# Regrouping the attention bursts between the units of a feed-forward pass: eight bursts instead of ten, value products behind score bursts, paired transposes in batch 1

## The chip, the cores and the metric

The kernel runs on one core of a Trainium2 chip. The metric is the device time of one execution in microseconds (us); lower is better.

## The reference

Two layers follow each other. The first is attention over 8 batches of 8 heads, 576 tokens and 64 values a head, with a mask: a token sees the tokens within 32 positions of it, eight global tokens are seen by all, and the global tokens see all. The second is a gated feed-forward layer on the 4608 tokens with 512 columns and 1536 hidden columns.

```python
def _attn_ref(q, k, v, global_idx):
    scores = scale * np.matmul(q, k.transpose(0, 1, 3, 2))
    mask = np.abs(pos[:, None] - pos[None, :]) <= window      # window = 32
    mask = mask | is_global[:, None] | is_global[None, :]
    scores = np.where(mask, scores, -1000000000.0)
    ...
    return np.matmul(attn, v)

def _moe_ref(x, w_gate, w_val, w_out):
    g = x @ w_gate
    silu = g * (1.0 / (1.0 + np.exp(-g)))
    return silu * (x @ w_val) @ w_out
```

## The kernel before

**The feed-forward part sets the pace.** It works on nine chunks of 512 tokens. A chunk is 16 units, written out by `ffn`: twelve gate units (four matmuls with `wg_sb`, four with `wv_sb`, each 128x512; then ScalarE's tanh and two VectorE products that make `h`), and four output units (twelve matmuls into `po`, a copy to `osb` by ScalarE, and a store). The loop at the end of the kernel runs through all units and counts them with `n`. Behind unit `n` it emits whatever stands in `gaps[n]`. In this text such a place is a **slot**, and what is emitted there on TensorE is a **burst**. The schedule is manual: every engine executes in the order in which the program emits.

**The attention of batch b is a list of steps** in `attention(b)`, dealt out to slots.

- `step_T` transposes k and q of two heads on TensorE (batches 1 and 2; from batch 3 on `transpose_qk` does it with DMA transposes on SP's queue).
- `step_GT`, `step_S2`, `step_SG`, `step_P2T` and `step_AV2` are the parts for the global tokens. `step_P2T` transposes on TensorE, and for batches 4 to 7 (`b >= XP`) with a DMA on SP's queue.
- `step_S(u)`, "score u", u = 0 to 4: sixteen small matmuls into `ps_s` (eight for u = 4), the exponential `pe` on ScalarE, and the mask product `pt` on VectorE.
- `step_AV(tp)`, "value tp", tp = 0 to 3: two matmuls with `gvt` and sixteen with `va` and its copy `vb`, shifted by 64 rows, into `ps_av`. Then VectorE normalises (`den`, its reciprocal, and the product `xa`). Values 0 and 1 use the masks of scores 0 and 1, values 2 and 3 those of scores 2 and 3. `step_AV8`, the tail product, does the last 64 tokens with score 4.
- `step_X(tp)` brings `xa` into `xT`, the input of the feed-forward part: four TensorE transposes and a ScalarE copy for batches 0 and 1, a DMA transpose on SP's queue from batch 2 (`b >= XB`). `step_X8` does so for the tail.

`vb()` copies `va` into `vb` with two DMAs on SP's queue, at the fourth place of batch 1's list, which is slot 5. They wait for the loads of v, which GpSimd issues in the order of the program.

**PSUM.** The pools `psc` (tag "sc") and `pm` (tag "m") hold one tile each, of 4 KB a partition[...]. Whoever takes the tile next waits until its last reader is done. [...] In `step_S` score 4 of batch 2 takes `pm`, the other scores after batch 0 take `psc`. `step_AV` places the values:

```python
            elif b < XQ:
                pool, tag = (psc, "sc") if tp and (b < XB or tp % 2) else (pm, "m")
            else:
                pool, tag = pm, "m"
```

**Where the steps land.** Batch 1 starts its list at slot 2, batch 2 at slot 15, one group a slot. Score 2 is then at slot 9 in batch 1 and at slot 22 in batch 2. Batches 3 to 7 deal their ten groups (one of them empty) over a whole chunk, group i in slot `o + 1 + (16 * i) // 10`, with `o = 16 * (b - 1)`: counted from `o`, score 2 is at 9, score 3 with value 0 at 10, value 1 at 12, score 4 with value 2 at 13, value 3 with the tail at 15. Slots 0 to 11 follow gates, slots 12 to 15 follow outputs.

Of the kernel before, what the change touches and what calls it, by code (L numbers as in the profile page):

```python
# [10 lines left out]
BF16 = mybir.dt.bfloat16  # L11
# [6 lines left out]
P = 128  # L18


def bc(ap, dims):

    return bass.AP(tensor=ap.tensor, offset=ap.offset, ap=[ap.ap[0]] + dims)
# [3 lines left out]
def kernel(  # L27
# [11 lines left out]
    nc = tc.nc  # L39

    B, H, S, D = q.shape
# [8 lines left out]
    HP = H // 2  # L50
# [4 lines left out]
    XB = 2  # L55
    XP = 4
# [11 lines left out]
    work = ctx.enter_context(tc.tile_pool(name="work", bufs=2))  # L68
# [3 lines left out]
    psc = ctx.enter_context(tc.tile_pool(name="psc", bufs=1, space=bass.MemoryType.PSUM))  # L72
    pm = ctx.enter_context(tc.tile_pool(name="pm", bufs=1, space=bass.MemoryType.PSUM))
# [73 lines left out]
    ident = const.tile([P, P], BF16)  # L147
# [23 lines left out]
    def clear(i):  # L171
# [10 lines left out]
        out=oh16.rearrange("p h a r -> p (h a r)"),  # L182
        in_=ident.rearrange("p (a g) -> p a g", g=NG), axis=AX.X, op=ALU.add,
# [3 lines left out]
        out=p8, in_=ident.rearrange("p (a g) -> p g a", g=NG), axis=AX.X, op=ALU.add  # L187
# [11 lines left out]
        out=tmp8h, in0=dmask.rearrange("p h r -> p (h r)"), in1=i8_f, op=ALU.mult  # L199
# [4 lines left out]
        out=gidx_f, in_=gidx_i64.bitcast(I32).rearrange("p (a b) -> p a b", b=2)[:, :, 0]  # L204
# [8 lines left out]
        out=hrow, in0=hrow, scalar1=float(S), scalar2=gcol, op0=ALU.mult, op1=ALU.add  # L213
# [4 lines left out]
        out=mka, in_=oh16.rearrange("p h a r -> p a r h"), axis=AX.X, op=ALU.add  # L218
# [6 lines left out]
        out=thr, in0=asel, scalar1=R2 + 0.25, scalar2=-0.25, op0=ALU.mult, op1=ALU.add  # L225
# [3 lines left out]
        out=sgn, in0=asel, scalar1=2.0, scalar2=-1.0, op0=ALU.mult, op1=ALU.add  # L229
# [3 lines left out]
        out=thi, in0=asel[:, 0:1], scalar1=1e6, scalar2=0.5, op0=ALU.mult, op1=ALU.add  # L233
# [25 lines left out]
    xT = wpool.tile([P, NCC, NT], BF16)  # L259

    def load_wgv(i):
# [13 lines left out]
        out=band, in_=band, compare_op=ALU.is_ge, fill=0.0,  # L275
# [3 lines left out]
        out=band, in_=band, compare_op=ALU.is_ge, fill=0.0,  # L279
# [60 lines left out]
    def attention(b):  # L340
        kT = kT_bufs[b % 2]
        va = va_bufs[b % 2]
        st = {}
# [139 lines left out]

        def step_S(u):
            hg, t0 = ((0, 0), (1, 0), (0, 4), (1, 4), (None, 8))[u]
            pool, tag = (pm, "m") if b == 0 and u in (2, 3) or b == 2 and u == 4 else (psc, "sc")
            ps = pool.tile([P, 2, 512], FP32, tag=tag, name="ps_s")
            if hg is None:
                slots = [(hp, hp, 8) for hp in range(HP)]
            else:  # L490
                slots = [(4 * i + tl, 2 * hg + i, t0 + tl) for i in range(2) for tl in range(4)]
            for slot, hp, t in slots:
                for par in range(2):
                    r = 64 * par
                    nc.tensor.matmul(  # L495
                        out=ps[:, par, 64 * slot : 64 * slot + 64],
                        lhsT=kT[r : r + 64, hp, 64 * t : 64 * t + P],
                        rhs=qTs[b][r : r + 64, hp, 64 * t : 64 * t + 64],
                        start=True, stop=True,
                    )  # L500
            ns = len(slots)
            pe = ppool.tile([P, 2, ns, 64], BF16, tag="pe", name="pe", bufs=3)
            nc.scalar.activation(  # L503
                out=pe, in_=ps[:, :, 0 : 64 * ns].rearrange("p r (s c) -> p r s c", c=64),
                func=AF.Exp, scale=SCALE,
            )
            pt = ppool.tile([P, 2, ns, 64], BF16, tag="p", name="pt")
            st["p", u] = pt
            mult = lambda: nc.vector.tensor_tensor(  # L509
                out=pt.rearrange("p r s c -> p (r s) c"),  # L510
                in0=pe.rearrange("p r s c -> p (r s) c"),
                in1=bc(band, [[0, 2 * ns], [1, 64]]), op=ALU.mult,
            )
            if b == 0:
                st["p*", u] = mult
            else:
                mult()
# [16 lines left out]
            )  # L534

        def step_AV(tp):
            st["xa", tp] = work.tile([P, H, D], BF16, tag="xa", name="xa", bufs=3)
            if b == 0:
                pool, tag = (pm, "m") if tp % 2 else (psc, "sc")
            elif b < XQ:  # L540
                pool, tag = (psc, "sc") if tp and (b < XB or tp % 2) else (pm, "m")
            else:
                pool, tag = pm, "m"
            full = pool.tile([P, 2, 512], FP32, tag=tag, name="ps_av")
            ps = full[:, :, 0 : 4 * W].rearrange("p g (h c) -> p g h c", c=W)
            for hg in range(2):
                r = slice(64 * hg, 64 * hg + 64)
                nc.tensor.matmul(  # L548
                    out=ps[:, hg], lhsT=st["pg"][r, P * tp : P * tp + P],
                    rhs=st["gv"][r].rearrange("p h r c -> p (h r) c"),  # L550
                    start=True, stop=False, skip_group_check=True,
                )
            for hg in range(2):
                pt = st["p", 2 * (tp // 2) + hg]
                for hl in range(4):
                    for e in range(2):
                        nc.tensor.matmul(  # L557
                            out=ps[64 * e : 64 * e + 64, hg, hl, :],
                            lhsT=pt[:, hl % 2, 4 * (hl // 2) + 2 * (tp % 2) + e, :],
                            rhs=(va if e == 0 else st["vb"])[:, tp, 4 * hg + hl, :],  # L560
                            start=False, stop=(hl == 3), skip_group_check=True,
                        )
            if b == 0:
                st["xa*", tp] = lambda: normalise(ps, st["xa", tp], 8)
            else:
                normalise(ps, st["xa", tp], 8)
# [25 lines left out]
        def step_X(tp):  # L592
# [18 lines left out]
            c0 = S * b + P * tp  # L611
            nc.scalar.copy(out=xT[:, :, c0 : c0 + P], in_=ps)

        def step_X8():
            if b >= XB:
                c0 = S * b + 512
                for g in range(2):
                    nc.sync.dma_start_transpose(
                        out=xT[:, 2 * g : 2 * g + 2, c0 : c0 + 64],
                        in_=st["xa8"][64 * g : 64 * g + 64].rearrange("p h d -> p (h d)"),  # L620
                    )
                return
            ps = mtile([P, 2, P], BF16, "ps_x8")
            for i in range(2):
                nc.tensor.transpose(
                    out=ps[:, i, :],
                    in_=st["xa8"][:, 2 * i : 2 * i + 2, :].rearrange("p h d -> p (h d)"),
                    identity=ident,
                )
            c0 = S * b + 512  # L630
            nc.scalar.copy(
                out=xT[:, :, c0 : c0 + 64].rearrange("p (g i) c -> p i g c", g=2),
                in_=ps.rearrange("p i (g c) -> p i g c", g=2),
            )
# [11 lines left out]
        L = lambda f, *a: (lambda: f(*a))  # L646
        if b == 0:
# [19 lines left out]
            [L(step_S2), L(step_SG)],  # L667
            [L(step_P2T), L(step_S, 0)],
            [L(step_S, 1), L(step_AV2)],
            [L(step_S, 2)],  # L670
            [L(step_S, 3), L(step_AV, 0)],
            [L(step_AV, 1), L(step_X, 0)],
            [L(step_AV, 2), L(step_X, 1)],
            [L(step_AV, 3), L(step_X, 2)],
            [L(step_X, 3), L(step_S, 4)],
        ]
        end = [[L(step_AV8)], [L(step_X8)]]
        if b < XQ:
            return [
# [1 line left out]
                *([[L(step_T, 2)], [L(step_GT), L(step_T, 3), vb]] if b == 1 else  # L681
                  [[L(step_GT), L(step_T, 2)], [L(step_T, 3), vb]]),
            ] + mid + end
        return [
            [L(step_GT), vb],
            [L(step_S2), L(step_SG)],
            [L(step_S, 0), L(step_P2T)],
            [],
            [L(step_S, 1), L(step_AV2)],
            [L(step_S, 2)],  # L690
            [L(step_S, 3), L(step_AV, 0), L(step_X, 0)],
            [L(step_AV, 1), L(step_X, 1)],
            [L(step_S, 4), L(step_AV, 2), L(step_X, 2)],
            [L(step_AV, 3), L(step_AV8), L(step_X, 3), L(step_X8)],
        ]


    def ffn(t0, n):
# [102 lines left out]
    gaps = {i: [] for i in range(9)}  # L801
# [23 lines left out]
    for b in range(XQ, B):  # L825
        steps = attention(b)
        o = 16 * (b - 1)
        for i, g in enumerate(steps):
            slot = o + 1 + (16 * i) // len(steps)
            gaps[slot] = gaps.get(slot, []) + g  # L830
        if b > XQ:
            tr_at[b] = o - 16 + 5
        if b > 4:
            cast_at[b] = o - 32 + 8
        v_at[b] = o - 16 + 2
        g_at[b] = o - 16 + 6
        m_at[b] = o - 16 + 13
# [4 lines left out]
    n = 0  # L842
# [38 lines left out]
```

## Time and profile before

| | |
|---|---|
| median of 11 runs | 369.67 us (367.06 to 370.54) |
| the profiled execution: its time | 365.74 us |
| the profiled execution: span of its instructions | 364.0 us |
| TensorE matmul busy | 346.1 us, 95% |
| VectorE busy | 233.8 us, 64% |
| ScalarE busy | 153.1 us, 42% |
| GpSimd busy | 97.4 us, 27% |

The profile is one execution. Busy times are unions of an engine's instructions, and matmuls overlap in their pipeline, so the cost of a group of matmuls is read from the end of the group before to its own end. A wait is an idle stretch of an engine with the instruction that ended it. In the timeline rows the columns are start, duration, engine, line, operation, what it writes and reads, and how many were merged into the row.

### The profile page before, as it was taken

The page shows a single profiled execution, that of the slowest core. Times are in us where ns is not written, and L with a number is a line of the kernel's source. Part 1 is how long each engine was busy: PE and PEld are TensorE (multiplying, and loading weights), DVE is VectorE, ACT ScalarE, POOL GpSimd, SP SyncE. Part 2 cuts the span into 40 slices and gives each one's busy share as a digit, 9 for nine tenths or more (in the row PEclk, how much of TensorE's full clock was granted, in tenths as well). Part 3 has the DMA queues.
Part 4 walks back from the last instruction along what each step waited for, and adds up shares of the span by engine and source line. Part 5 has one row for each costly group of instructions (what it writes and reads, how often), then busy time and mean ns, then how long its engine had stood idle before and what let it go on. Part 6 is the DMA issues. An engine that isn't in the chain of part 4 may idle for free.

```text
span 364.0 us, 7818 instructions
## 1 busy us (share of the span) xinstructions
PE 346.1 (95%) x3177; PEld 170.9 (47%) x3226; DVE 233.8 (64%) x469; ACT 153.1 (42%) x238; POOL 97.4 (27%) x114
## 2 busy tenths in 40 slices
PE   3769999999999999999999999999999999999996
PEld 2546544554444444444444444444444444444444
DVE  6665786368934884588548854885488638724850
ACT  5635673467324551355225532552254333323322
POOL 7925545934544001540245024100000000000000
PEclk9989999999999999999999999999999999999999
DMA  7999999999999927999899998932350131011002
GB/s 105 137 207 204 134 191 200 178 202 134 155 167 201 176 52 116 138 153 162 140 135 139 141 150 145 167 68 60 115 87 0 45 117 23 0 59 59 0 14 104
DMA packets 141636, 43.51 MB, mean 120 GB/s; under 512 B 126368, under 2 KB 135840, under 8 KB 141600
## 3 DMA queue, kind: packets, MB, share of 16 engines
q0 software_dynamic: 93824, 19.40, 62.7%
q1 hardware_dynamic: 47776, 23.60, 31.3%
q8 instruction: 25, 0.41, 0.5%
q14 instruction: 11, 0.09, 0.1%
HBM read 38.28 MB, written 15.34 MB: 147 GB/s over the span
## 4 chain that ended last, share of the span: by engine, by line
PE 92%; DMA 3%; DVE 2%; issue 1%; ACT 1%; POOL 0%; POOLq 0%; SPq 0%
PE pg L713 26%; PE po L774 25%; PE pv L713 25%; PE ps_s L495 3%; PE ps_av L557 3%; DMA vb<-va 2%; PE ps_av L548 1%; PE ps_t L377 1%; DMA k_bf<-in_k_dram 1%; PE ps_av L464 1%; PE ps_s L429 1%; PE po L761 1%; PE pg L731 1%; PE ps_x L606 1%; PE pv L731 1%
## 5 line engine op out<-in xcount | busy, mean ns | idle before, releaser
L713 PE MATMUL pg<-xT,wg_sb 128*128 128x512 bf16 x389 | 106.0, 380 | 2.0 <-issue 0.3
L713 PE MATMUL pv<-xT,wv_sb 128*128 128x512 bf16 x415 | 107.2, 379 | 0.3
L746 DVE SCALAR_TENSOR_TENSOR gv<-th,pg 128x512 bf16<-128x512 bf16 x107 | 73.3, 685 | 40.1 <-ACT th L744 39.5
L744 ACT ACTIVATE th<-pg 128x512 bf16<-128x512 f32 x107 | 63.9, 598 | 79.0 <-PE pg L713 70.2
L774 PE MATMUL po<-wo_sb,h 128*128 128x512 bf16 x410 | 92.8, 379 | 1.2 <-issue 1.0
L750 DVE TENSOR_TENSOR h<-gv,pv 128x512 bf16<-128x512 bf16 x107 | 73.6, 688 | 11.5 <-PE pg L713 0.5
L713 PEld LDWEIGHTS <-wv_sb 128*128 128x128 bf16 x424 | 41.5, 98 | 50.0
L774 PEld LDWEIGHTS <-h 128*128 128x128 bf16 x420 | 39.9, 98 | 46.4
L102 POOL DMA_DIRECT2D va<-in_v_dram x40 | 35.2, 988 | 95.6 <-PE ps_av L557 87.1
L713 PEld LDWEIGHTS <-wg_sb 128*128 128x128 bf16 x424 | 37.0, 98 | 40.9 <-issue 1.7
L779 ACT ACTIVATE osb<-po 128x512 f32<-128x512 f32 x35 | 20.9, 597 | 81.3 <-PE po L774 76.4
L503 ACT ACTIVATE pe<-ps_s 128x1024 bf16<-128x1024 f32 (+1 forms) x40 | 37.5, 938 | 18.6 <-PE ps_s L495 18.6
L509 DVE TENSOR_TENSOR pt<-pe,band 128x1024 bf16<-128x1024 bf16 (+1 forms) x40 | 25.5, 638 | 20.8 <-ACT pe L503 20.3
L524 DVE TENSOR_REDUCE den<-ps_av 128x8 f32<-128x16 f32 (+1 forms) x40 | 6.7, 169 | 35.7 <-PE ps_av L557 33.2
L530 DVE TENSOR_TENSOR xa<-ps_av,den 128x512 bf16<-128x512 f32 (+1 forms) x40 | 25.5, 638 | 1.6 <-DMA xT<-xa 0.3
L495 PEld LDWEIGHTS <-kT 64*128 64x128 bf16 x576 | 11.2, 97 | 15.9 <-issue 14.8
L495 PE MATMUL ps_s<-qT,kT 64*128 64x64 bf16 x576 | 16.0, 195 | 1.1 <-ACT pe L503 1.1
L557 PE MATMUL ps_av<-vb,pt 128*64 128x66 bf16 x256 | 14.4, 199 | 1.5 <-DMA vb<-va 1.5
L557 PE MATMUL ps_av<-va,pt 128*64 128x66 bf16 x256 | 14.7, 199 | 0.0
L109 POOL DMA_DIRECT2D qf<-in_q_dram x5 | 14.0, 2801 | 0.0
L557 PEld LDWEIGHTS <-pt 128*64 128x64 bf16 x512 | 11.1, 111 | 5.8 <-DMA vb<-va 1.6
L109 POOL DMA_DIRECT2D kf<-in_k_dram x5 | 11.4, 2285 | 7.4 <-DMA qf<-in_q_dram 7.1
(123 smaller groups left out, 213.7 us busy)
## 6 DMA issues: line engine op xcount, KB each, us to landing
out_dram<-osb SPq DMA_DIRECT2D x35, 256.0 KB, 2.2
vb<-va SPq DMA_DIRECT2D x14, 264.0 KB, 4.6
va<-in_v_dram POOLq DMA_DIRECT2D x24, 128.0 KB, 18.2
kf<-in_k_dram POOLq DMA_DIRECT2D x5, 576.0 KB, 10.4
qf<-in_q_dram POOLq DMA_DIRECT2D x5, 576.0 KB, 18.3
k_bf<-in_k_dram POOLq DMA_DIRECT2D x6, 288.0 KB
q_bf<-in_q_dram POOLq DMA_DIRECT2D x6, 288.0 KB, 4.3
va<-in_v_dram POOLq DMA_DIRECT2D x16, 96.0 KB, 7.8
```

Of the source, the lines that this page charges most:

```text
L102: nc.gpsimd.dma_start(out=va[lo:hi, u, :, 0:D], in_=vs[t0 + lo : t0 + hi])
L109: nc.gpsimd.dma_start(out=t, in_=src[b].rearrange("h s d -> s h d"))
L495: nc.tensor.matmul(out=ps[:, par, 64 * slot : 64 * slot + 64], lhsT=kT[r : r + 64, hp, 64 * t : 64 * t + P], rhs=qTs[b][r : r + 64, hp, 64 ...
L503: nc.scalar.activation(out=pe, in_=ps[:, :, 0 : 64 * ns].rearrange("p r (s c) -> p r s c", c=64), func=AF.Exp, scale=SCALE,)
L509: mult = lambda: nc.vector.tensor_tensor(out=pt.rearrange("p r s c -> p (r s) c"), in0=pe.rearrange("p r s c -> p (r s) c"), in1=bc(band, ...
L530: nc.vector.tensor_tensor(out=xa.rearrange("p (g h) d -> p g h d", g=g), in0=bc(ps, pst + [[1, D]]), in1=bc(den, [[4, g], [1, 4], [0, D]]) ...
L557: nc.tensor.matmul(out=ps[64 * e : 64 * e + 64, hg, hl, :], lhsT=pt[:, hl % 2, 4 * (hl // 2) + 2 * (tp % 2) + e, :], rhs=(va if e == 0 els ...
L713: nc.tensor.matmul(out=ps[:, 0:n], lhsT=w[:, cc, P * fc : P * (fc + 1)], rhs=xT[:, cc, t0 : t0 + n], start=(cc == 0), stop=(cc == NCC - 1),)
L744: nc.scalar.activation(out=th[:, 0:n], in_=pg[:, 0:n], func=AF.Tanh, scale=0.5)
L746: nc.vector.scalar_tensor_tensor(out=gv[:, 0:n], in0=th[:, 0:n], scalar=1.0, in1=pg[:, 0:n], op0=ALU.add, op1=ALU.mult,)
L750: nc.vector.tensor_tensor(out=st["h"][:, fc, 0:n], in0=gv[:, 0:n], in1=pv[:, 0:n], op=ALU.mult)
L774: nc.tensor.matmul(out=po, lhsT=st["h"][:, fc, P * ts : P * (ts + 1)], rhs=wo_sb[:, fc, :], start=(fc == 0), stop=(fc == NFC - 1),)
```

## The change

In **batches 3 to 7** the list becomes a table of slots: eight bursts instead of nine that are not empty. Value 0 joins score 2 (slot 9), value 1 joins score 3 (slot 11), value 2 stays with score 4 (now slot 12), value 3 stays with the tail (now slot 14). The DMA transpose of `step_P2T` is emitted at slot 2 for batches 4 to 7.

In **batch 1** value 0 joins score 2 and value 1 joins score 3. A new step `step_X01(n)` transposes two `xa` tiles into one `psc` tile, and one ScalarE copy brings both to `xT`. The second such pair stands in one group with score 4. The list is one group shorter.

In **batch 2** the same merges are made, value 3 joins score 4, and the list is two groups shorter. Score 4 of batch 2 moves to `psc`. For batches 1 and 2 only value 2 takes `psc`; the other values take `pm`. The pool of `xa` has four buffers instead of three.

```diff
-            pool, tag = (pm, "m") if b == 0 and u in (2, 3) or b == 2 and u == 4 else (psc, "sc")
+            pool, tag = (pm, "m") if b == 0 and u in (2, 3) else (psc, "sc")
...
-            st["xa", tp] = work.tile([P, H, D], BF16, tag="xa", name="xa", bufs=3)
+            st["xa", tp] = work.tile([P, H, D], BF16, tag="xa", name="xa", bufs=4)
...
-                pool, tag = (psc, "sc") if tp and (b < XB or tp % 2) else (pm, "m")
+                pool, tag = (psc, "sc") if tp == 2 else (pm, "m")
...
+        def step_X01(n):
+
+            ps = psc.tile([P, 2, 2, HP, P], BF16, tag="sc", name="ps_x")
+            for i in range(2):
+                for hp in range(HP):
+                    nc.tensor.transpose(
+                        out=ps[:, i, 0, hp, :],
+                        in_=st["xa", 2 * n + i][:, 2 * hp : 2 * hp + 2, :].rearrange(
+                            "p h d -> p (h d)"
+                        ),
+                        identity=ident,
+                    )
+            c0 = S * b + 2 * P * n
+            nc.scalar.copy(
+                out=xT[:, :, c0 : c0 + 2 * P].rearrange("p h (i c) -> p i h c", i=2),
+                in_=ps[:, :, 0],
+            )
...
             [L(step_S2), L(step_SG)],
             [L(step_P2T), L(step_S, 0)],
             [L(step_S, 1), L(step_AV2)],
-            [L(step_S, 2)],
-            [L(step_S, 3), L(step_AV, 0)],
-            [L(step_AV, 1), L(step_X, 0)],
-            [L(step_AV, 2), L(step_X, 1)],
-            [L(step_AV, 3), L(step_X, 2)],
-            [L(step_X, 3), L(step_S, 4)],
+            [L(step_S, 2), L(step_AV, 0)],
+            [L(step_S, 3), L(step_AV, 1)],
+            [L(step_AV, 2)],
+            [L(step_AV, 3), L(step_X01, 0)],
+            [L(step_X01, 1), L(step_S, 4)],
+        ] if b < XB else [
+            [L(step_S2), L(step_SG)],
+            [L(step_P2T), L(step_S, 0)],
+            [L(step_S, 1), L(step_AV2)],
+            [L(step_S, 2), L(step_AV, 0), L(step_X, 0)],
+            [L(step_S, 3), L(step_AV, 1), L(step_X, 1)],
+            [L(step_AV, 2), L(step_X, 2)],
+            [L(step_S, 4), L(step_AV, 3), L(step_X, 3)],
         ]
...
-        return [
-            [L(step_GT), vb],
-            [L(step_S2), L(step_SG)],
-            [L(step_S, 0), L(step_P2T)],
-            [],
-            [L(step_S, 1), L(step_AV2)],
-            [L(step_S, 2)],
-            [L(step_S, 3), L(step_AV, 0), L(step_X, 0)],
-            [L(step_AV, 1), L(step_X, 1)],
-            [L(step_S, 4), L(step_AV, 2), L(step_X, 2)],
-            [L(step_AV, 3), L(step_AV8), L(step_X, 3), L(step_X8)],
-        ]
+        return {
+            1: [L(step_GT), vb],
+            2: [L(step_S2), L(step_SG)] + ([L(step_P2T)] if b >= XP else []),
+            4: [L(step_S, 0)] + ([] if b >= XP else [L(step_P2T)]),
+            7: [L(step_S, 1), L(step_AV2)],
+            9: [L(step_S, 2), L(step_AV, 0), L(step_X, 0)],
+            11: [L(step_S, 3), L(step_AV, 1), L(step_X, 1)],
+            12: [L(step_S, 4), L(step_AV, 2), L(step_X, 2)],
+            14: [L(step_AV, 3), L(step_AV8), L(step_X, 3), L(step_X8)],
+        }
...
-        for i, g in enumerate(steps):
-            slot = o + 1 + (16 * i) // len(steps)
-            gaps[slot] = gaps.get(slot, []) + g
+        for i, g in steps.items():
+            gaps[o + i] = gaps.get(o + i, []) + g
```

## The prediction

> **What bounds the kernel now.** I read the page first: busy time by engine, then the granted clock and the list of TensorE's waits.
>
> ```profile
> PE 346.1 (95%) x3177; PEld 170.9 (47%) x3226; DVE 233.8 (64%) x469; ACT 153.1 (42%) x238; POOL 97.4 (27%) x114
> ```
> ```profile
> PE ps_t L357 <- DMA k_bf<-in_k_dram: 6.3, 2, 6.0
> PE ps_av L557 <- DMA vb<-va: 1.5, 1, 1.5
> PE ps_g L395 <- DVE kqm L249: 1.2, 1, 1.2
> PE ps_s L495 <- ACT pe L503: 1.1, 1, 1.1
> ```
>
> TensorE is the bound: every long wait lies in the first 25 us, in batch 0. After it TensorE runs without a hole, so only two things can change the time: what a burst costs TensorE itself, and new waits. The timeline of TensorE in a later batch (start, duration) prices the bursts:
>
> ```profile
> 242.54 1.03 PE L713 MATMUL pv<-xT,wv_sb 128*128 128x512 bf16 x4
> 243.50 0.41 PE L495 MATMUL ps_s<-qT,kT 64*128 64x64 bf16 x16
> 243.84 1.04 PE L713 MATMUL pg<-xT,wg_sb 128*128 128x512 bf16 x4
> 244.72 1.03 PE L713 MATMUL pv<-xT,wv_sb 128*128 128x512 bf16 x4
> 245.68 0.41 PE L495 MATMUL ps_s<-qT,kT 64*128 64x64 bf16 x16
> ...
> 246.38 0.20 PE L557 MATMUL ps_av<-vb,pt 128*64 128x66 bf16 x1
> ...
> 248.24 2.75 PE L774 MATMUL po<-wo_sb,h 128*128 128x512 bf16 x12
> ```
>
> From end to end: a score burst alone takes 243.57 to 243.91, 0.34 us. Scores with a value product take 245.75 to 246.58, 0.83. A value product alone, after the output product ending 250.99, took to 251.59: 0.59. The gate unit behind a burst takes 1.83 (243.91 to 245.75); in a row of gates each takes 1.73. So a merge saves 0.34 + 0.59 - 0.83 = 0.10 in the burst and 0.10 in the unit behind it: **0.20 us for each burst that joins another**.
>
> [...] the 0.10 appears where 128*128 tiles give way to 64*128 or 128*64 and back. [...] the vb copies of batch 1 took 8 us beside weight loads, 4.7 in the median. [...] (busy us in the first number after the stretch, clock behind the engines):
>
> ```profile
> 21.70:25.11 3.41, 1.50 (x25) 0.95 (x26) 2.14 (x6) 0.58 (x1) 0.88 (x2) 1.00 1.22 236
> 25.11:28.52 3.41, 3.41 (x34) 2.42 (x34) 1.96 (x5) 0.58 (x1) 1.35 (x2) 0.50 1.25 204
> 18.28:21.70 3.42, 2.16 (x54) 1.45 (x54) 2.34 (x8) 2.05 (x2) 1.34 (x3) 1.00 1.16 180
> ```
>
> A window with 1.50 us busy was followed by half clock for 3.41 us; one with 2.16 was not.
>
> **The gain.** Batches 3 to 7: score 2, scores 3 with value 0 and value 1 (0.34 + 0.83 + 0.59, with 0.10 behind each) become two merged bursts: 0.20 each, 5 x 0.20 = 1.0 us. Batches 1 and 2, each burst with its 0.10 behind, in the same costs (four transposes behind a value product add 0.34 and leave no 0.10 behind them, four more 0.22; 24 transposes of q and k take 0.63, the tail product 0.48). Batch 1, score 2 to score 4: before 0.44 + 1.05 + 0.93 + 0.93 + 0.93 + 0.55 = 4.83, with a wait of 0.12 in it; after 0.93 + 0.93 + 0.69 + 1.15 + 0.76 = 4.46. Its tail steps meet batch 2's transposes elsewhere: before 1.09 + 0.84, after 0.58 + 0.84 + 0.73, so 0.22 more. Batch 2, score 2 to the tail: before 0.44 + 0.93 + 3 x 0.69 + 0.32 + 0.58 = 4.34, after 0.93 + 0.93 + 0.69 + 0.81 + 0.58 = 3.94. Net 0.37 - 0.22 + 0.40 = 0.55. Gain in all: **1.55 us**. Nothing is removed from TensorE; ACT has two copies of some 1.01 us for batch 1 (estimate: 372 ns at 256 columns and 585 at 512 give 0.83 ns a column) for four of 585. ACT is 42% busy and its copies end nothing, so 0.
>
> **New wait 1: vb of batch 1.** Its copies stay at slot 5, but value 0 moves from slot 10 to slot 9. The timeline at slot 10 and the issue on SP:
>
> ```profile
> 46.54 0.46 SPq L130 DMA_DIRECT2D vb<-va  x1
> ```
> ```profile
> DMA to landing us min/median/max: 7.9/8.0/8.0
> ```
> ```profile
> 54.51 0.22 PE L557 MATMUL ps_av<-va,pt 128*64 128x66 bf16 x1
> 54.63 0.22 PE L557 MATMUL ps_av<-vb,pt 128*64 128x66 bf16 x1
> ```
>
> The second copy lands at 46.54 + 8.0 = 54.54, and already holds the first product with vb by 0.12 us (54.51 to 54.63). The copies wait on POOL's v loads, which wait on transfers, not on TensorE, so they land no earlier. At slot 9 the burst would end at 51.95 + 0.83 = 52.78; held until 54.63 it ends at 55.07, as it does now at slot 10. **Cost 2.29 us.** Everything on TensorE queues behind it. Bounds: 0 if the copy lands by 52.5, 3 if it is 0.7 late.
>
> **New wait 2: one buffer for the transposes and score 4 of batch 1.** Before, transpose 3 is in pool pm and score 4 in psc. After, the pair X01(1) and score 4 stand in one burst and both take the single psc tile. Score 4 waits for ACT's copy, and all of TensorE for score 4. Before, at this place:
>
> ```profile
> 67.29 0.39 PE L606 MATMUL ps_x<-ident,xa 128*128 128x128 bf16 x4
> 67.49 0.60 ACT L779 ACTIVATE osb<-po 128x512 f32<-128x512 f32 x1 [2.00 <-PE po L774]
> 67.61 0.29 PE L495 MATMUL ps_s<-qT,kT 64*128 64x64 bf16 x8
> 67.98 0.58 ACT L612 COPY xT<-ps_x 128x512 bf16<-128x512 bf16 x1
> ```
>
> The copy starts 0.53 after the output product's end at 67.45 (behind osb), takes 1.01, release about 0.05: score 4 begins at +1.6 where its transposes end at +0.44. **Cost 1.15 us.** Bounds 0.9 to 1.3.
>
> **New wait 3: batch 2 with one gate between bursts.** Value 0, 1 and 3 take pm, value 2 takes psc: each waits for VectorE's normalisation of the one before. VectorE per slot: two products of a gate 1.51, mask 0.69, normalisation 1.1 = 3.3 us, against TensorE's 0.83 + 1.83 = 2.66. It falls behind. Rows of VectorE:
>
> ```profile
> 88.59 0.18 DVE L479 TENSOR_TENSOR gvt<-lo,gvt 128x4 bf16<-128x4 f32 x1
> ...
> 92.13 0.69 DVE L509 TENSOR_TENSOR pt<-pe,band 128x1024 bf16<-128x1024 bf16 x1
> ...
> 93.18 0.69 DVE L530 TENSOR_TENSOR xa<-ps_av,den 128x512 bf16<-128x512 f32 x1
> ```
>
> From mask start to xa end is 1.74 us. I carry the after order forward from slot 22 (gate end 88.53). gvt ends 88.77, value 0 wanted at 88.71: with about 0.05 us for the release, 0.1. Mask 2 from 90.07, so xa 0 ends 91.81; value 1 wanted at 91.50: 0.37. Then gate and mask again: xa 1 at 94.85, gate 24's products to 96.24, xa 2 at 97.22; score 4, in psc, wanted at 96.7: 0.5. xa 3 at 100.0; the tail product in pm wanted at 99.83: 0.2. **Cost 1.2 us**, bounds 0.6 and 1.8. Batch 1's same chain is covered by wait 1, in which VectorE catches up.
>
> **Later batches: nothing.** Two gates lie between slots 9 and 11. By the same working xa 1 ends at 251.17 and value 2, behind output product 0, is wanted at 251.55: cover 0.35 us; if gone, up to 0.3 x 5. SP's order stays vb, p2t, kT, qT, so the p2t transposes (slot 4 to 2) issue as now; the last transposes pass one store in later batches and two in batch 2, six osb buffers hide it. POOL's order is unchanged. The fourth xa buffer takes a wait off VectorE (0.3 us, off the path). An empty list entry costs 0.
>
> **Sum:** -1.55 + 2.29 + 1.15 + 1.2 = **+3.1 us** on the profiled time of 365.74 (span 364.0 and 1.7 around it). The median, 369.67, is 3.9 above that time; I add the same 3.1 to it: **372.8**.
>
> **Rivals.** *Half clock behind wait 1*: [...] 3.41 us at half speed lose 1.7: 374.5. [...] I take 0 for the main case. *The copy is in time*: if the 3.9 us that timed runs last longer lie on TensorE ahead of slot 9, the copy lands before it is wanted; wait 1 and its 0.12 go, batch 1 gets some 0.5 of batch 2's waits: -1.43 + 1.15 + 1.2 + 0.5 = +1.4, 371.1. Against: no such delay shows in the profiled run. *Faster*: if those 3.9 us are a half-clock stretch on batches 1 and 2 (52 to 100 us), ACT, VectorE and DMA keep their pace while each TensorE slot lengthens by up to 2.6 us; waits 1 to 3 vanish and -1.55 is left: 368.1. It decides once the granted clock there is below 0.9; the trace has 1.0. *The change does less than it says*: if two of three waits are covered, the rest cancels the gain: within 0.3% of 369.67.
>
> **How the numbers follow.** 0.3%, 1.1 us, is about what a measurement of this kernel can tell from no change. Main case 0.36, half clock 0.26, copy in time 0.18 (0.14 slower, 0.04 same), cancelled 0.08, faster 0.12. Slower 0.76, same 0.12, faster 0.12. The slower cases alone span 371.0 to 375.2. The range, 369.9 to 375.2, leaves out the faster case and half of the cancelled one.
>
> **What would show it.** Right: at slot 9 of batch 1 a hole of about 2 us ahead of a value product on vb; 1.1 us ahead of score 4 of batch 1, released by ACT's xT copy; four small holes at slots 22 to 26, released by VectorE; from batch 3 merged bursts of 0.83 and no hole. Half clock shows in the slice after 55 us. Wrong: no hole at 52 to 55 us, or holes in every later batch behind output product 0.

## The result, and the profile after

The changed kernel takes **372.12 us** in the median of 13 runs (370.13 to 374.98); the kernel before, run beside it, takes 368.20 (50 runs). The ratio is 1.0106, with a 95% interval of [1.0081, 1.0131]: slower by 3.9 us, 3.0 to 4.8. One further execution of the kernel before took 592 us at a mean granted clock of 0.572; it is left out of every comparison.

The profiled execution of the changed kernel has a span of 369.4 us, 5.4 more than before's 364.0. The first line of its page says that TensorE's work hardly grew:

```profile
PE 347.1 (94%) x3173; PEld 172.5 (47%) x3226; DVE 232.6 (63%) x469; ACT 153.4 (42%) x236; POOL 97.5 (26%) x114
```

Not all of the 5.4 us belongs to the change. The program is the same up to score 2 of batch 1, so both spans are read from score 1 on. The timeline of TensorE at score 1 of batch 1 and at the last output product, before:

```profile
49.31 0.41 PE L495 MATMUL ps_s<-qT,kT 64*128 64x64 bf16 x16
...
358.18 2.78 PE L761 MATMUL po<-wo_sb,h 128*128 128x256 bf16 x24
```

and after:

```profile
51.66 0.41 PE L495 MATMUL ps_s<-qT,kT 64*128 64x64 bf16 x16
...
363.52 2.78 PE L784 MATMUL po<-wo_sb,h 128*128 128x256 bf16 x24
```

From score 1 to the last end, before takes 49.31 to 360.96, 311.65 us. After takes 51.66 to 366.30, 314.64: **+2.99 us**. The other 2.35 us lie in the start-up; over the twelve profiles of this study score 1 began anywhere from 48.81 to 52.70. What goes with this spread is how fast TensorE runs in the start-up. A matmul of the same line and shape there takes 0.38 us before and 0.61 after (before first):

```profile
19.93 0.38 PE L336 MATMUL ps_w<-ones 128*128 128x512 bf16 x1 [0.16 <-issue]
```
```profile
22.85 0.61 PE L336 MATMUL ps_w<-ones 128*128 128x512 bf16 x1
```

Eleven of the twelve traces have a record of the granted clock. Its first stretch at full clock begins at 18.28 in the profile of before and at 31.31 in that of after. In the six profiles in which it begins by 26 us, score 1 stands at 48.81 to 50.50, and in the five in which it begins between 27 and 33 us, at 50.28 to 51.94. No run changed the start-up's clock by itself, so that the clock causes the spread is likely but not shown.

From here on "from score 1" means this stretch, and "from score 2" the same from score 2 of batch 1 (before 309.08, after 312.06).

TensorE's waits after the change (total, times, longest):

```profile
PE ps_av L557 <- DMA vb<-va: 2.4, 2, 1.5
PE ps_s L495 <- ACT xT L627: 1.1, 1, 1.1
...
PE ps_t L377 <- DVE qT L386: 0.6, 1, 0.6
PE ps_s L495 <- DVE xa L530: 0.5, 1, 0.5
...
PE ps_av L548 <- DVE xa L530: 0.2, 1, 0.2
...
PE ps_av L576 <- DVE xa L530: 0.2, 1, 0.2
```

The vb row holds 1.5 us of batch 0, there before as well, and a new wait; the other five rows are new. Now each place in the timeline (the bracket is the idle time ahead of a row and what ended it). Slot 9 of batch 1, TensorE:

```profile
54.24 0.41 PE L495 MATMUL ps_s<-qT,kT 64*128 64x64 bf16 x16
54.68 0.29 PE L548 MATMUL ps_av<-gvt,pg 64*128 64x264 bf16 x2
54.90 0.22 PE L557 MATMUL ps_av<-va,pt 128*64 128x66 bf16 x1
56.08 0.22 PE L557 MATMUL ps_av<-vb,pt 128*64 128x66 bf16 x1 [0.96 <-DMA vb<-va]
```

The first product with vb stands 0.96 us; from end to end the burst takes 2.21 instead of 0.83, so 1.38 us more. The second transposed pair of batch 1 and score 4:

```profile
67.88 0.61 PE L619 MATMUL ps_x<-ident,xa 128*128 128x128 bf16 x8
...
68.08 0.60 ACT L802 ACTIVATE osb<-po 128x512 f32<-128x512 f32 x1 [1.58 <-PE po L797]
...
68.57 1.01 ACT L627 COPY xT<-ps_x 128x1024 bf16<-128x1024 bf16 x1
...
69.63 0.29 PE L495 MATMUL ps_s<-qT,kT 64*128 64x64 bf16 x8 [1.14 <-ACT xT L627]
```

ScalarE copies an output to `osb` first, then the pair for 1.01 us, and only then does score 4 get the `psc` tile. From end to end this burst takes 1.88 us instead of 0.66 (the prediction's 0.76 less the 0.10 behind it): 1.22 more. Batch 2's second, fourth and last burst:

```profile
97.38 0.29 PE L548 MATMUL ps_av<-gvt,pg 64*128 64x264 bf16 x2 [0.19 <-DVE xa L530]
...
102.85 0.29 PE L495 MATMUL ps_s<-qT,kT 64*128 64x64 bf16 x8 [0.55 <-DVE xa L530]
...
105.62 0.30 PE L576 MATMUL ps_av<-gvt,pg 64*64 64x264 bf16 x2 [0.16 <-DVE xa L530]
```

From end to end four bursts of batch 2 are 0.14 (score 2 with value 0, no hole above 0.1), 0.36, 0.62 and 0.23 longer than the same bursts without a wait: 1.35 in all. And one wait that nobody had foreseen, at slots 15 and 16 (batch 2's transposes of q and k):

```profile
75.99 1.01 POOL L240 DMA_INDIRECT qg<-in_q_dram,gofs  x1 [0.30 <-issue]
76.12 0.42 PE L377 MATMUL ps_t<-ident,q_bf 96*64 96x96 bf16 x12
...
77.50 0.64 ACT L382 COPY kT<-ps_t 128x576 bf16<-128x576 bf16 x1 [0.81 <-PE pg L736]
...
78.17 0.76 DVE L386 COPY qT<-ps_t 128x576 bf16<-128x576 bf16 x1 [4.20 <-ACT kT L382]
...
78.99 0.41 PE L377 MATMUL ps_t<-ident,k_bf 96*64 96x96 bf16 x11 [0.61 <-DVE qT L386]
```

The transposes end at 76.54, yet ScalarE's copy of them starts at 77.50. So both copies are late, and the next transposes, which need the tile, stand 0.61 us (0.68 from end to end). From batch 3 on the merged bursts run without a hole:

```profile
137.99 0.41 PE L495 MATMUL ps_s<-qT,kT 64*128 64x64 bf16 x16
138.23 0.28 PE L548 MATMUL ps_av<-gvt,pg 64*128 64x264 bf16 x2
```

The balance from score 1: 1.38 + 1.22 + 1.35 + 0.68 = 4.63 of new waits, less before's 0.12 at slot 10, less 2.99 measured, leaves a gain of 1.52 us. That is what is left over, not a measurement; the version near the end of the experiments, with most of the waits gone, tests it. Of it 1.11 is seen by itself: from batch 3's first score to the end before takes 239.63 (121.33 to 360.96), after 238.52 (127.78 to 366.30).

### The profile page after: what moved, and what is told of

Read it like the earlier page. It is cut to its first block, busy times and chain, and to the rows that moved or that the text cites. A ratio compares the mean times of both kernels' runs of the same rounds, so it can differ in the third digit from the quotient of the medians.

```text
span 369.4 us, 7808 instructions
## 1 busy us (share of the span) xinstructions
PE 347.1 (94%) x3173; PEld 172.5 (47%) x3226; DVE 232.6 (63%) x469; ACT 153.4 (42%) x236; POOL 97.5 (26%) x114
## 4 chain that ended last, share of the span: by engine, by line
PE 78%; DMA 11%; DVE 5%; POOL 3%; issue 2%; ACT 1%; DVEq 0%; POOLq 0%
PE po L797 25%; PE pg L736 22%; PE pv L736 21%; DMA kg<-in_k_dram,gofs 4%; DMA wg_sb<-in_moe_w_gate_dram 3%; PE ps_av L557 2%; PE ps_s L495 2%; DMA vb<-va 2%; DMA va<-in_v_dram 2%; POOL va L102 1%; DVE h L773 1%; PE ps_av L548 1%; DVE gv L769 1%; DVE pt L509 1%; DVE xa L530 1%
## 5 line engine op out<-in xcount | busy, mean ns | idle before, releaser
L736 PE MATMUL pg<-xT,wg_sb 128*128 128x512 bf16 x397 | 104.9, 380 | 2.6 <-issue 1.1
L773 DVE TENSOR_TENSOR h<-gv,pv 128x512 bf16<-128x512 bf16 x107 | 73.6, 688 | 11.1
L736 PEld LDWEIGHTS <-wg_sb 128*128 128x128 bf16 x424 | 37.9, 98 | 42.8 <-issue 1.7
```

What stands on the lines that cost most here:

```text
L736: nc.tensor.matmul(out=ps[:, 0:n], lhsT=w[:, cc, P * fc : P * (fc + 1)], rhs=xT[:, cc, t0 : t0 + n], start=(cc == 0), stop=(cc == NCC - 1),)
L773: nc.vector.tensor_tensor(out=st["h"][:, fc, 0:n], in0=gv[:, 0:n], in1=pv[:, 0:n], op=ALU.mult)
```

## Experiments

Diffs are against the changed kernel, the first one's against the kernel before. Ratios are to the kernel before, on the same chip.

### The new order for batches 3 to 7 alone

```diff
-        for i, g in enumerate(steps):
-            slot = o + 1 + (16 * i) // len(steps)
-            gaps[slot] = gaps.get(slot, []) + g
+        for i, g in steps.items():
+            gaps[o + i] = gaps.get(o + i, []) + g
```

(and the table of slots as in the change; batches 1 and 2 and all pools stay as before)

> The kernel before, with the new table of slots for batches 3 to 7 alone; batches 1 and 2 as before. Theory (merges save 0.20 us each, all losses are waits in batches 1 and 2): from the start of score 2 of batch 1 to the last matmul 308.1 us (before 309.1, after 312.1), no hole of TensorE behind 100 us, time 1.0 us under before, ratio 0.997. Rival (the later batches lose too, value 2 waits for the normalisation behind output product 0): 309 us or more, with holes at slot 12 of each batch.

Measured: 366.74 us, ratio 0.9969 [0.9944, 0.9993], 1.1 us faster. The stretch from batch 3's first score to the end is 238.84, 0.79 shorter than before, with one hole of 0.26 in it. From score 2 it came to 309.72 instead of the 308.1 expected, because two holes lie in batches 1 and 2, whose order is here that of before: 0.51 for vb at slot 10, and 0.77 at slot 17, for the copies of the transposes of slot 16. The timeline there:

```profile
76.54 0.64 ACT L382 COPY kT<-ps_t 128x576 bf16<-128x576 bf16 x1 [1.71 <-PE pg L711]
...
77.77 0.23 PE L377 MATMUL ps_t<-ident,k_bf 96*64 96x96 bf16 x2 [0.77 <-ACT qT L386]
```

The hole of 0.26 waits for the DMA transpose of `step_P2T` in batch 4. It follows that the later batches bring their gain, and that the vb wait, and a wait for late copies of transposes, also occur in the order of before, in some executions. They are races, not waits that the change created. Value 0 a slot earlier makes the first one longer; whether the change makes the second likelier is not shown.

### Score 4 of batch 1 in the other pool

```diff
-            pool, tag = (pm, "m") if b == 0 and u in (2, 3) else (psc, "sc")
+            pool, tag = (pm, "m") if b == 0 and u in (2, 3) or b == 1 and u == 4 else (psc, "sc")
```

> The changed kernel, with score 4 of batch 1 in the pool pm instead of psc, nothing else. Theory: the hole of 1.14 us ahead of score 4 of batch 1 goes, and 310.9 us remain from score 2 of batch 1 to the last matmul (after 312.1). Rival (ScalarE's queue is the cause and the buffer only shows it: what stands behind the copy is late all the same): the hole moves to the tail product or to batch 2's first transposes, and 312 us remain.

Measured: 371.11 us, 1.0080 [1.0041, 1.0119]; from score 2 311.13 (after 312.06). TensorE at the same place:

```profile
67.44 0.61 PE L619 MATMUL ps_x<-ident,xa 128*128 128x128 bf16 x8
67.98 0.29 PE L495 MATMUL ps_s<-qT,kT 64*128 64x64 bf16 x8
```

The 1.14 us are gone: wait 2 is the shared tile. The stretch is shorter by 0.93 only, because three other waits moved too: slot 16 stands 1.59 here instead of 0.61, and slots 9 and 10 are 0.30 and 0.36 longer than without a wait, instead of 1.38 and nothing. At slot 9 vb is in time in this profile. What the value product waits for is `gvt`, which `step_AV2` of slot 8 hands to VectorE:

```profile
54.82 0.18 DVE L479 TENSOR_TENSOR gvt<-lo,gvt 128x4 bf16<-128x4 f32 x1
...
55.05 0.10 PEld L548 LDWEIGHTS <-pg 64*128 64x128 bf16 x2 [0.24 <-DVE gvt L479]
```

So behind the wait for vb at slot 9 there stands a second one of 0.30, and behind that VectorE's chain at slot 10, as in batch 2.

### The last loads of v for batch 1 issued earlier

```diff
-        load_v(1, range(0, 3))
+        load_v(1)
...
-        load_v(1, range(3, 5))
```

> The changed kernel, with the last two v loads of batch 1 issued ahead of batch 1's two mask products on GpSimd instead of behind them. Theory (the copy vb lands too late because GpSimd holds the v loads back): vb is issued some 3 to 6 us earlier, the wait of value 0 of batch 1 (1.38 us longer burst) goes, 310.7 us remain from score 2 of batch 1 to the last matmul; the mask products stay where they are. Rival (the transfer engines are full and the copy lands when it lands): the landing moves by less than 1 us and a wait of 0.5 us or more stays.

Measured: 369.86 us, 1.0042 [1.0025, 1.0058]. SP issued the two copies at 43.86 and 44.38 instead of 45.70 and 49.34, so it was the loads that they waited for, and vb was there at 53.20 instead of 56.08. But TensorE came to slot 9 2.5 us earlier too, so 0.65 us of idling stays, and slot 16 stands 1.31. From score 2 the profile takes 312.40, not 310.7. The timed runs gain 2.4 us on the changed kernel; the single profile doesn't show that gain.

### Batch 2 with two gates between its merged bursts

```diff
             [L(step_S, 3), L(step_AV, 1), L(step_X, 1)],
-            [L(step_AV, 2), L(step_X, 2)],
-            [L(step_S, 4), L(step_AV, 3), L(step_X, 3)],
+            [],
+            [L(step_S, 4), L(step_AV, 2), L(step_X, 2)],
+            [],
+            [L(step_AV, 3), L(step_X, 3)],
```

(and one empty entry ahead of score 3)

> The changed kernel, with batch 2's merged bursts two slots apart: score 2 with value 0 at slot 22, score 3 with value 1 at 24, score 4 with value 2 at 26, value 3 at 28, tail at 29; same pools. Theory (VectorE falls behind when one gate lies between the bursts, and the single PSUM tiles pass that on): the holes of 0.14, 0.36, 0.62 and 0.23 us go, 310.7 us remain from score 2 of batch 1 to the last matmul. Rival (each value waits for the normalisation ahead of it wherever it stands): at least 0.8 us of holes stay in batch 2, 311.5 us or more.

Measured: 371.78 us, 1.0102 [1.0065, 1.0138], no better than the change. The waits of 0.36, 0.62 and 0.23 are gone. The first, 0.14 at slot 22, stays: slots 21 and 22 are as in the change. And one hole took their place:

```profile
103.61 0.29 PE L495 MATMUL ps_s<-qT,kT 64*128 64x64 bf16 x8
104.59 0.29 PE L548 MATMUL ps_av<-gvt,pg 64*128 64x264 bf16 x2 [0.69 <-ACT pe L503]
```

My edit put value 2, which takes `psc`, behind score 4 in `psc`, in one burst: the same mistake as wait 2. This profile also has a vb wait of 2.0 and one of 1.7 at slot 16, so from score 2 it takes 313.82 instead of 310.7.

### The gathers of batch 3 issued later

Two gathers of GpSimd (`kg` and `qg` for batch 3) run at the time of the late copies of slot 15. Here they stand four places later.

```diff
-        g_at[b] = o - 16 + 6
+        g_at[b] = o - 16 + (10 if b == XQ else 6)
```

> The changed kernel, with GpSimd's two gathers of global rows for batch 3 behind the casts of batch 4 instead of ahead of them. In all runs so far with a hole ahead of batch 2's second transposes (0.6 to 1.7 us), TensorE's last transpose of slot 15 told of its end late, while those gathers ran at 74 to 77 us. Theory (a gather on GpSimd holds back TensorE's signal): no hole at slot 16; late signals instead where the gathers stand now, some 88 to 91 us; 0.6 us less than after from score 2 of batch 1 to the last matmul, apart from wait 1. Rival (the late signal belongs to the place, ScalarE's copies of the tail and of k in a row): the hole stays at 0.6 us or more with the gathers gone.

Measured: 371.30 us, 1.0094 [1.0064, 1.0125]. Slot 15, timeline:

```profile
77.22 0.42 PE L377 MATMUL ps_t<-ident,q_bf 96*64 96x96 bf16 x12
...
77.68 0.66 ACT L382 COPY kT<-ps_t 128x576 bf16<-128x576 bf16 x1
```

The copy follows the transposes' end (77.64) at once, and slot 16 has no hole. The other half of the expectation did not come. The gathers now run at 80.96 to 83.30, the transposes of slot 17 end at 82.68, in the second gather, and their copy is not late either:

```profile
82.26 0.42 PE L377 MATMUL ps_t<-ident,q_bf 96*64 96x96 bf16 x12
82.30 1.00 POOL L240 DMA_INDIRECT qg<-in_q_dram,gofs  x1 [0.30 <-issue]
...
82.72 0.64 ACT L382 COPY kT<-ps_t 128x576 bf16<-128x576 bf16 x1 [0.89 <-PE ps_t L377]
```

So this run does not show that a gather holds the signal back. From score 1 it still takes 316.39, because vb was late by 1.81 us, and what came then was a stretch at a granted clock of 0.50. Busy time in the two stretches (first number after the stretch is its length, the second TensorE's busy time; the clock stands behind the engines):

```profile
53.69:57.11 3.42, 1.61 (x23) 0.91 (x22) 2.43 (x6) 0.85 (x1) 0.99 (x1) 1.00 1.21 207
57.11:60.52 3.41, 3.41 (x40) 1.60 (x39) 1.78 (x4) 1.62 (x2) 2.30 (x3) 0.50 1.31 204
```

TensorE was busy for 1.61 us of the first, and the second, 3.41 us, ran at half clock; 1.7 us, half of it, is the estimate of what that costs. By sum, in bursts from end to end (slot 9 0.79 longer than in the change, slot 16 0.68 shorter, batch 2's tail 0.18 longer): 314.64 + 0.79 - 0.68 + 0.18 + 1.7 = 316.6; measured 316.39.

### Batch 1 one slot later from score 2 on

```diff
             [L(step_S, 1), L(step_AV2)],
+            [],
             [L(step_S, 2), L(step_AV, 0)],
```

> The changed kernel, with batch 1's list from score 2 on one slot later (slot 9 empty, score 2 with value 0 at slot 10, the tail again with batch 2's first transposes). Theory (value 0 at slot 9 is ahead of its copy vb): the wait on vb, 0.3 to 2.4 us at slot 9 in the runs so far, is at most 0.3; the wait of score 4 on ScalarE's copy, 1.1 us, stays, as do batch 2's four; time 1 us under after. Rival (the copy lands later whenever TensorE has more to do ahead of it): a wait of 0.5 us or more on vb stays.

Measured: 368.17 us, 1.0016 [0.9993, 1.0038]. TensorE at slots 10 and 11:

```profile
57.46 0.22 PE L557 MATMUL ps_av<-vb,pt 128*64 128x66 bf16 x1
...
60.31 0.29 PE L548 MATMUL ps_av<-gvt,pg 64*128 64x264 bf16 x2 [0.23 <-DVE xa L530]
```

No wait for vb, nor at slot 16; a small new one at value 1, a hole of 0.23 and 0.41 from end to end; waits 2 and 3 as in the change. The tail of batch 1 is back with batch 2's first transposes, as before the change, which by the prediction's working saves 0.22. By sum 314.64 - 1.38 - 0.68 + 0.41 - 0.22 = 312.77 from score 1; measured 312.75. The timed ratio falls by 0.90 points, 3.3 us (some 2.1 to 4.5 by the two intervals). This profile is shorter by 1.9 us.

### Batch 2 spread, with value 2 in the other pool

```diff
-                pool, tag = (psc, "sc") if tp == 2 else (pm, "m")
+                pool, tag = (psc, "sc") if tp == 2 and b < XB else (pm, "m")
```

(and batch 2's list as in "Batch 2 with two gates between its merged bursts")

> The changed kernel, with batch 2's merged bursts two slots apart as in the run before, and value 2 of batch 2 in pm, since in psc it stood behind score 4 of its own burst (a hole of 0.69 us there). Theory (one gate between bursts is too little for VectorE): no hole over 0.1 us in batch 2 from score 2 to the tail, where after has 1.35 us of waits. Rival (the waits move on): holes of 0.3 us or more stay at slots 24 to 29.

Measured: 369.96 us, 1.0064 [1.0045, 1.0084], 1.5 us less than the change in the timed runs. Batch 2 has no hole over 0.1 left (0.14 from end to end stays at slot 22): the other three parts of wait 3 are VectorE's chain with one gate between bursts. From score 1 the profile takes 315.25 nevertheless, with vb late by 1.85 and half clock after it:

```profile
52.76:56.17 3.41, 1.55 (x37) 0.94 (x36) 2.42 (x6) 1.08 (x2) 0.99 (x1) 1.00 1.18 223
56.17:59.59 3.42, 3.42 (x12) 0.96 (x12) 1.76 (x4) 0.60 (x1) 1.37 (x2) 0.50 1.30 202
```

By sum: 314.64 + 0.87 (slot 9) - 1.21 (batch 2) - 0.68 + 1.7 = 315.3. Slot 16 has no hole here, though the gathers stand where they stood in the change.

### All of it together

The four edits behind which a wait was gone: score 4 in `pm`, batch 1 one slot later, batch 2 spread with value 2 in `pm`, the gathers later.

> The changed kernel with the remedies together: batch 1 from score 2 one slot later, its score 4 in pm, batch 2 spread with value 2 in pm, the gathers of batch 3 later. Theory: no hole over 0.3 us behind 45 us; from score 1 of batch 1 to the last matmul 309.8 us, where before has 311.65 and after 314.64; ratio to before 0.995. Rival (removing one wait exposes another): holes of 0.5 us or more in batches 1 or 2, ratio 0.998 or more.

Measured: **364.99 us**, 0.9938 [0.9916, 0.9960]: faster than both kernels. That is 2.3 us (1.5 to 3.1), more than the prediction's gain of 1.55; part of it may be waits and half-clock stretches of the kernel before itself (next but one section), which no run separates. In this profile TensorE was early (score 1 at 48.81), so vb was late even at slot 10, by 1.26, and 311.40 from score 1 stands where 309.8 was expected. In the stretch around it TensorE was busy for 2.16 us, and the next one ran at full clock:

```profile
51.66:55.08 3.42, 2.16 (x29) 0.96 (x28) 3.06 (x6) 1.62 (x2) 1.30 (x2) 1.00 1.16 222
55.08:58.49 3.41, 3.41 (x59) 1.84 (x60) 2.57 (x6) 1.40 (x2) 0.91 (x2) 1.00 1.28 204
```

### The same with the loads of v first, and that at slot 9

The first adds this edit to the version above, as in the third experiment; the second then takes the empty entry of batch 1 out again, so that score 2 and value 0 stand at slot 9.

```diff
-        load_v(1, range(0, 3))
+        load_v(1)
...
-        load_v(1, range(3, 5))
```

> The run with all remedies, and the last two v loads of batch 1 ahead of its mask products on GpSimd. That run still had 1.26 us of wait on vb at slot 10, because TensorE began early. Theory (two chains race to value 0: transfers to vb, TensorE to its slot): vb lands some 1.5 to 2.5 us earlier, no hole over 0.3 us behind 45 us, from score 1 of batch 1 to the last matmul 310 us, ratio to before 0.991. Rival (the transfer engines set the landing): the wait on vb stays at 0.7 us or more, ratio 0.994.

Measured: 365.48 us, 0.9940 [0.9920, 0.9961]. TensorE's waits:

```profile
PE ps_av L556 <- DMA vb<-va: 1.8, 1, 1.8
...
PE ps_av L547 <- DVE xa L529: 0.2, 1, 0.2
```

The first lies in batch 0. Behind 45 us no hole is over 0.23, and from score 1 it takes 310.34, where 310 was expected. The whole is 311.65 - 310.34 = 1.31 us shorter than before. From end to end two small waits are still in it, 0.41 at value 1 of batch 1 and 0.14 at slot 22, and the place of batch 1's tail saves the 0.22 of the working: 1.31 + 0.55 - 0.22 = 1.64 us for the merges of the change with no new wait, before's 0.12 in it; the prediction's gain was 1.55. The balance of the change's profile gave 1.52 + 0.12, the same. The timed ratio of 0.991 that was expected did not come.

> As the run before it, but value 0 of batch 1 at slot 9 as in the change (no empty slot). Theory (the slot decides, 2.2 us earlier on TensorE): a wait of 0.5 to 2 us on vb at slot 9, ratio 0.5% above the run before it, with a half-clock window in some executions. Rival (with the v loads first the copy is in time for slot 9 too): no wait, and the ratio of the run before it.

Measured: 365.79 us, 0.9947 [0.9927, 0.9967]; vb is late by 0.73 at slot 9, and from score 1 it takes 311.24. The half per cent by which it was expected to be slower than the version before it did not come: in time the last three can't be told apart.

### What the clock of the timed runs adds

Each execution has its mean granted clock. It counts half clock only after the first stretch at full clock; the slow start-up is not in it, as the profile of after shows, with a mean of 1.0 though its first stretch at full clock begins at 31.31. One half-clock stretch of 3.41 us lowers it by an estimated 0.005 (half of 3.41 out of 365); in before's profile, with one such stretch and the last 0.97 us at 0.50, the mean is 0.994. Executions at 0.995 or less, with the vb wait in the kernel's profile:

| kernel | executions at 0.995 or less | vb idle in batch 1, us |
|---|---|---|
| before (beside the experiments) | 33 of 114 | under 0.1 |
| batches 3 to 7 alone | 4 of 22 | 0.51 |
| after | 12 of 15, three of them at 0.991 | 0.96 |
| score 4 in `pm` | 5 of 7 | none |
| loads of v first | 3 of 22 | 0.65 |
| batch 2 spread | 2 of 6 | 2.0 |
| gathers later | 6 of 8 | 1.81 |
| one slot later | 1 of 14 | none |
| batch 2 spread, value 2 in `pm` | 20 of 22 | 1.85 |
| all four together | 0 of 11 | 1.26 |
| all, loads of v first | 1 of 8 | none |
| the same, value 0 at slot 9 | 4 of 22 | 0.73 |

Where value 0 stays at slot 9 and the loads stay late, 45 of 58 executions stand at 0.995 or less (five kernels of the table); where the change's list of batch 1 stands a slot later, 2 of 33. The idle of the one profile does not tell the share. The clock of a timed run does not say where its half clock lay. Two profiles, above, have a stretch of it behind slot 9, but in the profiles of before and of "gathers later" one lies in the start-up, at 25.11 and 26.39. After's three executions at full clock average 370.87 us, all fifteen (the timed runs, the profiled one and one more) 372.10; before's are 367.52 and 367.83. So an estimate of 0.9 us of the slowdown goes with the larger share of half-clock executions. It stands on three executions, and whatever else such executions have in common is in it.

## Why the prediction was right, and where it was not

**The gain: right.** Predicted 1.55 us, 1.43 without before's 0.12. The balance gives 1.52, the version with the loads of v first the same, and batches 3 to 7 show 1.11 for 1.0 predicted. "Later batches: nothing" held in the changed kernel's profile, with no hole there; with batches 3 to 7 alone there was one of 0.26, for `step_P2T`'s transpose, which the prediction had put at nothing.

**Wait 1: right place, mis-sized in the profile.** Predicted 2.29, measured 1.38. The working took slot 9 and the landing from before's profile. In after's, TensorE came to score 1 2.35 us later and the copy, issued at 49.34 instead of 46.54, landed some 1.45 later: 2.29 - 2.35 + 1.45 = 1.39. "They land no earlier" held. The step that failed is the use of both times of one profile as if they were fixed; they drift against each other from one execution to the next. Idle times for vb from none to 2.0 us at slot 9, in kernels with the same loads and order up to it, show the spread. With vb in time, 0.30 for `gvt` remains, which the working had priced in batch 2 but not here. One slot's delay saves 3.3 us in the timed runs, half clock included; the profile of after may have been a mild case, but the lower end of the interval, 2.1, is close to the 1.9 of the profiles.

**Half clock: the term set to 0 should not have been.** It was kept as a rival at 1.7 us; that it could come behind wait 1 was my estimate, from one pair of stretches in before's profile (1.50 us busy of 3.41, then a clock of 0.50). It came behind slot 9 in two of the profiles, where the sums with 1.7 come out within 0.3 us, and 12 of 15 executions of after have a mean clock of 0.995 or less. In the main case it belonged with its mean, which the groups of executions put at about 0.9 us, an estimate. When a wait of this length has half clock behind it is not shown: it came behind waits of 1.81 and 1.85 us, and not behind one of 2.0.

**Wait 2: right.** Predicted 1.15, measured 1.22 (hole 1.14); it went with the shared tile.

**Wait 3: right.** Predicted 0.1, 0.37, 0.5, 0.2, measured 0.14, 0.36, 0.62, 0.23: 1.35 for 1.2. All but the first 0.14 went when two gates stood between bursts, and a hole of 0.69 came while value 2 still shared a tile with score 4.

**Slot 16: missed.** 0.68 us in the profile. The kernel with the old order in batches 1 and 2 shows such a wait a slot later, so how much of it the change adds to the mean is open, and so is its cause.

**The sum.** In the profile, +2.99 for +3.1 is partly luck: wait 1 fell 0.91 short, and slot 16 put 0.68 of it back, waits 2 and 3 another 0.22. In the timed runs, +3.9 (3.0 to 4.8) for +3.1 leaves 0.8, about what half clock adds; but +3.1 lies within the interval, and how long wait 1 is there in the mean was not measured by itself. The predicted 372.8 stood on the median of 369.67 from 11 runs; with more runs the kernel before is at 368.2. The base was 1.5 too high and the step 0.8 too low, so that 372.12 comes this near to 372.8 is luck too.

**The rivals.** "Faster" needed a long stretch at a clock below 0.9 over batches 1 and 2; no profile with a record of the clock has more there than single stretches of 3.41 us at 0.50. "The copy is in time" did not come in the changed kernel's profile, though its premise, TensorE late at slot 9, did: 2.35 us. The copy was late as well. One slot's delay shows about what it would have been: +0.6 us (-0.3 to 1.4), where the rival had +1.4. "Does less than it says" fell, since each of the three waits was there.

## What to carry to other kernels

A burst that joined another saved some 0.2 us here, but all that it needs must be there one slot earlier: go through its transfers, the tile that both parts take, and the engine chain between two bursts, and give each the slot back that it lacks. Where a wait depends on a transfer and on an engine that both drift from execution to execution, treat it as a spread and give its tail its own price, here the half clock. A gain of 0.4% on a kernel like this needs the waits out first: the merges cost 1.1% with them, and 0.6% was gained once most of them were gone.

## What the runs showed of the hardware

**Half clock behind some of the waits.** In three profiles a stretch of 3.41 us at full clock in which TensorE was busy for 1.50 us (before), 1.55 ("batch 2 spread, with value 2 in the other pool") and 1.61 ("the gathers of batch 3 issued later") was followed by 3.41 us at a clock of 0.50. Stretches with 2.16 (before, and "all of it together") and 2.10 ("batch 2 with two gates between its merged bursts") were followed by one at 1.00. So was one with 1.82, in the profile of "score 4 of batch 1 in the other pool", where the wait at slot 16 lies:

```profile
76.49:79.90 3.41, 1.82 (x31) 1.16 (x30) 2.12 (x3) 2.09 (x4) 0.51 (x1) 1.00 2.14 199
79.90:83.31 3.41, 3.41 (x39) 1.67 (x37) 2.33 (x5) 2.06 (x4) 2.15 (x1) 1.00 1.46 223
```

The stretch with 2.10 and the next, with 2.73, share a wait of 2.0 us for vb; the next and the one behind it, with 3.41 us busy, ran at 1.00. Waits of 1.81 and 1.85 us had half clock behind them. So in these profiles a wait of this length cost an estimated 1.7 us more (half of 3.41) or nothing, and what decides between the two was not shown.

**Late copies behind transposes, cause open.** In seven profiles ScalarE's copy of transposed k started 0.5 to 2.1 us after TensorE's transposes had ended, and ScalarE was idle for 0.5 to 1.9 us of it (after: transposes' end 76.54, ScalarE free at 76.70, copy at 77.50). The transposes were those of slot 15, 16 or 17 and ended between 73.6 and 78.9 us, while GpSimd's two gathers for batch 3 were being issued. Elsewhere at slots 15 to 18 the copy starts 0.04 us after their end. But in three profiles transposes ended within one of these gathers and the copy was on time: 0.07 us with the gathers in their old place ("batch 2 spread, with value 2 in the other pool"), and 0.04 with the gathers later ("the gathers of batch 3 issued later", and "all, loads of v first"). So a gather at that moment is not enough, and the cause stays open.
